# The end of the last batch in an attention and gated-MLP kernel: another order of products, statistics and writes

## The chip, the cores and the metric

The kernel runs on one core of a Trainium2 chip. A core has a matrix engine (TensorE, PE in the profile), a vector engine (VectorE, DVE), a scalar engine (ScalarE, ACT), a general-purpose engine (GpSimd, POOL) and a sync engine (SyncE, SP) that here only issues transfers. They run side by side, each in its own fixed order, and wait for one another through semaphores. Sixteen DMA engines move data. The metric is the device time of one execution in microseconds (us), lower is better.

## The reference

There are 8 batches of 576 tokens. Attention with 8 heads of 64 keeps only the scores within `tau` of the row's maximum; its result, 512 wide, is the input x of a gated MLP:

```python
h = np.maximum(x @ w_in, 0.0)                      # 512 -> 1024
u, v = h[..., :512], h[..., 512:]
v_n = (v - mean(v)) / np.sqrt(var(v) + 1e-06)      # over the 512 features of a token
v_s = einsum('ts,bsd->btd', w_spatial, v_n) + b_spatial[None, :, None]
out = (u * v_s) @ w_out                            # 512 -> 512
```

The spatial product runs over the tokens, so no row of the output can be finished before all tokens of v_n are there.

## The kernel before

Attention is worked off in steps, each of a block of 128 tokens for two heads: scores on TensorE, the maximum on VectorE, the exponentials and masks on ScalarE and VectorE, a DMA transpose of the probabilities, and the product with v. The order is written out by hand: a string of short tokens for each batch (`ORDER`) and four strings for the end (`LAST`). A token names one piece of work, and `run_token` (the long `elif` chain) emits its instructions at that place on whichever engines it uses. After the colon stands how many batches back it belongs to. The MLP of a batch runs in the gaps of the attention of the next two, but the last batch has no attention to hide behind: its MLP is `last_gmlp`, and the tokens of `LAST` are emitted around its parts, which are separated by `yield`.

The pieces that matter here:

- `P`, `i` and `p` are the product with v, the reciprocal of the row sums (L531) and the normalised rows xn (L534, VectorE). xn is held in two halves of four heads each, m = 14 and m = 15 for the last batch.
- `X0` sends the half m = 14 through a DMA transpose issued on SP (L555) and gives the contraction parts 0 and 1 of xT. `XP2`, `XP3` (L576) transpose the half m = 15 on TensorE, and `xp2`, `xp3` evict it with ScalarE (L416, L584) and VectorE (L585): parts 2 and 3 of xT.
- `o0` to `o3` are the last but one batch's output products (L767). `eo0` to `eo3` evict them (L778, even blocks on ScalarE, odd ones on VectorE) and issue the write on SP (L782). `s4` and `es4` are its spatial product for the last 64 tokens and the gating of it (L743, L755, VectorE).
- `u0` to `u4` and `eu0` to `eu4` are the last batch's u products (L709, L714) and their Relu on ScalarE (L412).

`last_gmlp` makes, block by block of 128 tokens (c = 0 to 3, and c = 4 with 64), the value product over four contraction parts f (L934; L627 for block 4, together with the output of the previous batch's last 64 rows, L630, in `ends`), its Relu on ScalarE (L941), mean and variance with bn_stats and bn_aggr on VectorE (L943, L945), and 1/sqrt on GpSimd in two calls (L957). After the next `yield` it forms the normalised values vn (L965, L968, L971). Then come the spatial products, `gate`, on half a bank of 256 tokens at a time (L982), each followed by VectorE's multiplication with u (L984), `gate_rest` for the last 64 tokens (L991), and the output products (L1001) with ScalarE's copy (L1003) and a write (L1004) from SP or, for odd blocks, from GpSimd's queue. `output_halves` does the last 64 rows as two halves whose writes are issued on SP and ScalarE (L1019).

The results of matmuls lie in eight banks, handed out in turn by `bank()`: six of one pool and two of another. A bank can be written again only when its last reader is done.

Of the kernel before, what the change touches and what calls it, by code (L numbers as in the profile page):

```python
# [9 lines left out]
F32 = mybir.dt.float32  # L10
BF16 = mybir.dt.bfloat16
# [4 lines left out]
ALU = mybir.AluOpType  # L16
ACT = mybir.ActivationFunctionType
# [145 lines left out]
    "C15:1 es1:2 OUT3:3 A15:1 E17:1 T13:1 s3:2 "),  # L163
(
# [3 lines left out]
(  # L168
    "u0:1 eu0:1 u1:1 eu1:1 "),
(  # L170
    "u2:1 eu2:1 u3:1 eu3:1 u4:1 eu4:1 ")]
WAYS = [
    "nananaanananaaanaa",
    "naaaaanananaaanaaa",
# [10 lines left out]
def kernel(  # L185
# [17 lines left out]
    nc = tc.nc  # L203
    B, H, S, D = q.shape
    assert (B, H, S, D) == (8, 8, 576, 64)
    scale = 0.125
# [3 lines left out]
    P = 128  # L210
# [3 lines left out]
    small = ctx.enter_context(tc.tile_pool(name="small", bufs=6))  # L214
# [3 lines left out]
    vr = ctx.enter_context(tc.tile_pool(name="vr", bufs=4))  # L218
    orr = ctx.enter_context(tc.tile_pool(name="orr", bufs=1))
    oo = ctx.enter_context(tc.tile_pool(name="oo", bufs=2))  # L220
    sqr = ctx.enter_context(tc.tile_pool(name="sqr", bufs=1))
# [12 lines left out]
    mhalf = const.tile([P, 1], F32, name="mhalf")  # L234
# [23 lines left out]
    w_in = const.tile([P, 4, 1024], BF16, name="w_in")  # L258
# [128 lines left out]
    def bank(dtype=F32, n=512):  # L387
        if wide:

            turn[0] += 1  # L390
            if turn[0] % 8 not in (2, 3):
                return wide[0].tile([P, n], dtype, name="t")
        return ps_f.tile([P, n], dtype, name="f")
# [164 lines left out]
    def x_of(b, f, cols):  # L558

        at = 640 * (f % 2)  # L560
        return xt_of(b)[:, f // 2, at + cols.start:at + cols.stop]
# [58 lines left out]
    us, gs = {}, {}  # L620
    pair_o = {}

    def ends(t, b):


        for f in range(4):
            nc.tensor.matmul(out=t[0:64], lhsT=rest_of(b, f), rhs=w_in[:, f, 512:1024],  # L627
                             start=(f == 0), stop=(f == 3))
            if b:
                nc.tensor.matmul(out=t[64:128], lhsT=gs[b - 1][:, f, 512:576],  # L630
                                 rhs=w_o[:, f, :], start=(f == 0), stop=(f == 3))
# [286 lines left out]
    def stage():  # L918

        t = ld_ring[len(staged) // 3 % 2][len(staged) % 3]  # L920
        half = len(staged) // 6 % 2
        staged.append(t)
        return t.rearrange("p h c d -> p (h c d)")[:, 512 * half:512 * half + 512]

    def last_gmlp(b):

        vn = vn_ring[b % 2]
        norms = []
        var = small.tile([P, 5], F32, name="var")
        vrel, mvs = [], []  # L930
        for c in range(5):
            t = bank()
            for f in range(4 if c < 4 else 0):
                nc.tensor.matmul(out=t, lhsT=x_of(b, f, slice(c * P, (c + 1) * P)),  # L934
                                 rhs=w_in[:, f, 512:1024], start=(f == 0), stop=(f == 3))
            if c == 4:
                ends(t, b)
            n = P if c < 4 else 64
            vrel.append(vr.tile([P, 512], F32, name="vrel") if c < 4 else
                        orr.tile([P, 512], F32, name="o"))  # L940
            nc.scalar.activation(out=vrel[c][:n], in_=t[:n], func=ACT.Relu)  # L941
            st = small.tile([P, 6], F32, name="st")
            nc.vector.bn_stats(out=st[:n], in_=vrel[c][:n])  # L943
            mvs.append(small.tile([P, 2], F32, name="mv"))
            nc.vector.bn_aggr(out=mvs[c][:n], in_=st[:n])  # L945
            if c == 4:
                nc.vector.memset(var[64:128, 4:5], 1.0)
                o = stage()
                nc.scalar.copy(out=o[64:128], in_=t[64:128])
                nc.sync.dma_start(out=out[b - 1, 512:576, :], in_=o[64:128])  # L950
            nc.vector.tensor_scalar(out=var[:n, c:c + 1], in0=mvs[c][:n, 1:2], scalar1=1e-6,
                                    scalar2=1.0, op0=ALU.add, op1=ALU.mult)
            if c in (2, 4):

                lo = 0 if c == 2 else 3
                rs = small.tile([P, 5], F32, name="rstd")
                nc.gpsimd.tensor_tensor(out=rs[:, lo:c + 1], in0=var[:, lo:c + 1],  # L957
                                        in1=mhalf.broadcast_to([P, c + 1 - lo]), op=ALU.pow)
                for d in range(lo, c + 1):
                    norms.append((d, rs[:, d:d + 1]))  # L960
        yield
        for d, rs in norms:
            n = P if d < 4 else 64
            nm = small.tile([P, 1], F32, name="nm")
            nc.vector.scalar_tensor_tensor(out=nm[:n], in0=mvs[d][:n, 0:1], scalar=-1.0,  # L965
                                           in1=rs[:n], op0=ALU.mult, op1=ALU.mult)
            if d == 3:
                nc.scalar.activation(out=vn[:n, d, :], in_=vrel[d][:n], func=ACT.Identity,  # L968
                                     scale=rs[:n], bias=nm[:n])
            else:  # L970
                (nc.gpsimd if d == 0 else nc.vector).tensor_scalar(  # L971
                    out=vn[:n, d, :], in0=vrel[d][:n], scalar1=rs[:n], scalar2=nm[:n],
                    op0=ALU.mult, op1=ALU.add)
        yield
        g = mw.tile([P, 4, S], BF16, name="gT")
        rows = out[b, 0:512, :].rearrange("(p c) n -> p c n", c=4)

        def gate(f, half):
            t = bank()
            cols = slice(256 * half, 256 * half + 256)  # L980
            for c in range(5):
                nc.tensor.matmul(out=t[:, 0:256], lhsT=vn[:, c, f * P:(f + 1) * P],  # L982
                                 rhs=wsT[:, c, cols], start=(c == 0), stop=(c == 4))
            nc.vector.tensor_tensor(out=g[:, f, cols], in0=t[:, 0:256], in1=us[b][:, f, cols],  # L984
                                    op=ALU.mult)

        def gate_rest():
            t = bank()
            for h in range(4):
                for c in range(5):  # L990
                    nc.tensor.matmul(out=t[:, h * 64:h * 64 + 64],  # L991
                                     lhsT=vn[:, c, h * P:(h + 1) * P],
                                     rhs=wsT[:, c, 512:576], start=(c == 0), stop=(c == 4))
            nc.vector.tensor_tensor(out=g[:, :, 512:576],
                                    in0=t[:, 0:256].rearrange("p (f s) -> p f s", f=4),
                                    in1=us[b][:, :, 512:576], op=ALU.mult)

        def output(c):
            t, o = bank(), stage()
            for f in range(4):  # L1000
                nc.tensor.matmul(out=t, lhsT=g[:, f, c * P:(c + 1) * P], rhs=w_o[:, f, :],  # L1001
                                 start=(f == 0), stop=(f == 3))
            nc.scalar.copy(out=o, in_=t)  # L1003
            (nc.sync, nc.gpsimd)[c % 2].dma_start(out=rows[:, c, :], in_=o)  # L1004

        def output_halves(c):
            ts, o = [bank(), bank()], stage()
            at = [slice(0, P)] * 2 if c < 4 else [slice(0, 64), slice(64, P)]
            n = P if c < 4 else 64
            for f in range(4):  # L1010
                for h in range(2):
                    nc.tensor.matmul(out=ts[h][at[h], 0:256], lhsT=g[:, f, c * P:c * P + n],
                                     rhs=w_o[:, f, 256 * h:256 * h + 256],
                                     start=(f == 0), stop=(f == 3))
            for h in range(2):
                cols = slice(256 * h, 256 * h + 256)
                (nc.scalar.copy, nc.vector.tensor_copy)[h](out=o[at[h], cols],
                                                           in_=ts[h][at[h], 0:256])
                (nc.sync, nc.scalar)[h].dma_start(  # L1019
                    out=rows[:, c, cols] if c < 4 else out[b, 512:576, cols], in_=o[at[h], cols])  # L1020

        for f in range(4):
            gate(f, 0)
        gate_rest()
        gate(0, 1)
        output(0)
        gate(1, 1)
        output(1)
        gate(2, 1)
        gate(3, 1)  # L1030
        output(2)
        output(3)
        output_halves(4)
        yield

# [175 lines left out]
```

## Time and profile before

| what | us |
|---|---|
| median of three runs | 437.54 |
| lowest and highest of them | 434.55 and 438.42 |
| the profiled execution, its own time | 439.63 |
| span of the profiled execution | 437.9 |
| transpose of xT, part 0 and 1: issued, landed | 409.22, 414.13 |
| first value product of the last batch | 414.18 |
| first and last bn_stats | 415.88, 420.05 |
| last matmul begins (output halves) | 432.37 |
| last writes issued | 433.37 to 433.52 |

The granted TensorE clock of the profiled execution is 0.994 of full speed. Three things help in reading its lines. A time is the start from the beginning of the span. In a line of the timeline the bracket gives how long the engine had been idle before and what ended that idle time; `x16` is a group of 16 instructions that follow one another. And the chain of work that ended last is walked back from the last instruction: at each step to whatever released it, or to the instruction before it on the same engine. Of the profiled span's last stretch, 433.1 to 437.9, nothing is computed any more; the last writes land and the program ends.

### The profile page before, as it was taken

The page shows a single profiled execution, that of the slowest core. Times are in us where ns is not written, and L with a number is a line of the kernel's source. Part 1 is how long each engine was busy: PE and PEld are TensorE (multiplying, and loading weights), DVE is VectorE, ACT ScalarE, POOL GpSimd, SP SyncE. Part 2 cuts the span into 40 slices and gives each one's busy share as a digit, 9 for nine tenths or more (in the row PEclk, how much of TensorE's full clock was granted, in tenths as well). Part 3 has the DMA queues.
Part 4 walks back from the last instruction along what each step waited for, and adds up shares of the span by engine and source line. Part 5 has one row for each costly group of instructions (what it writes and reads, how often), then busy time and mean ns, then how long its engine had stood idle before and what let it go on. Part 6 is the DMA issues. An engine that isn't in the chain of part 4 may idle for free.

```text
span 437.9 us, 12915 instructions
## 1 busy us (share of the span) xinstructions
PE 406.9 (93%) x4998; PEld 257.2 (59%) x5048; DVE 376.3 (86%) x689; ACT 383.5 (88%) x584; POOL 168.6 (39%) x374
## 2 busy tenths in 40 slices
PE   8778889989999999988999999999999999999895
PEld 4446655565755666565565666656656656555553
DVE  6889989898989889987889898988998998998482
ACT  4899989999999988998988999999999989998252
POOL 1244426583345611545233713356125621253021
PEclk9899999999999999999999999999999999999999
DMA  7999999999899999999989999999999997959803
GB/s 196 219 248 189 219 251 245 204 222 210 199 245 174 259 207 174 200 201 185 257 140 251 219 174 245 213 221 207 221 191 239 199 229 171 193 104 215 178 30 109
DMA packets 224637, 88.17 MB, mean 201 GB/s; under 512 B 195648, under 2 KB 220352, under 8 KB 224576
## 3 DMA queue, kind: packets, MB, share of 16 engines
q1 hardware_dynamic: 224048, 86.49, 97.6%
q8 instruction: 40, 0.66, 0.6%
q0 software_dynamic: 160, 0.52, 0.3%
q10 hardware_dynamic: 368, 0.33, 0.2%
q14 instruction: 21, 0.17, 0.1%
HBM read 32.79 MB, written 9.44 MB: 96 GB/s over the span
## 4 chain that ended last, share of the span: by engine, by line
PE 64%; ACT 12%; DVE 8%; DMA 6%; issue 5%; POOL 4%; SPq 1%; POOLq 0%; ACTq 0%; DVEq 0%
PE s L816 27%; PE f L738 6%; ACT e L874 5%; PE f L434 5%; PE f L496 5%; DVE s L850 5%; PE f L709 4%; PE f L642 4%; PE f L767 4%; DMA pT<-p 3%; ACT e L871 2%; ACT p L909 2%; PE f L491 2%; DMA xT<-xn 1%; PE f L627 1%
## 5 line engine op out<-in xcount | busy, mean ns | idle before, releaser
L850 DVE TENSOR_REDUCE s<-s 128x2 f32<-128x1152 f32 x144 | 196.2, 1362 | 22.3 <-PE s L816 18.7
L816 PE MATMUL s<-qkT 64*64 64x160 f32 (+1 forms) x2304 | 173.0, 418 | 13.3 <-ACT e L874 6.3
L816 PEld LDWEIGHTS s<-qkT 64*64 64x64 f32 x2304 | 107.6, 133 | 71.8 <-ACT e L874 18.1
L874 ACT ACTIVATE e<-s,negm 128x576 f32<-128x576 f32 x192 | 133.1, 744 | 9.6 <-DVE negm L856 7.1
L909 ACT ACTIVATE p<-e 128x1152 f16<-128x1152 f32 x96 | 111.6, 1173 | 0.7 <-PE s L816 0.2
L871 ACT ACTIVATE e<-s,negm 128x576 f16<-128x576 f32 x96 | 66.8, 746 | 6.4 <-DVE negm L856 4.5
L320 POOL CAST v<-vl 128x512 bf16<-128x512 f32 x32 | 20.2, 632 | 78.3 <-PE s L816 66.1
L496 PE MATMUL f<-v,pT 128*128 128x65 bf16 x984 | 44.6, 194 | 0.0
L496 PEld LDWEIGHTS <-pT 128*128 128x128 f16 x1024 | 41.9, 98 | 2.2 <-issue 0.2
L293 POOL COPY qn<-ql 128x512 f32<-128x512 f32 x31 | 20.4, 660 | 49.5 <-PE s L816 40.6
L902 DVE TENSOR_TENSOR p<-e 128x576 int32<-128x576 int32 x48 | 36.9, 772 | 0.7 <-PE s L816 0.5
L738 PE MATMUL f<-wsT,vn 128*128 128x512 bf16 x125 | 32.2, 380 | 0.4
L491 PE MATMUL f<-v,pT 128*128 128x130 bf16 x123 | 27.3, 222 | 3.9 <-DMA pT<-p 3.7
L694 POOL TENSOR_SCALAR vn<-vrel,rs,nm 128x512 bf16<-128x512 f32 (+1 forms) x35 | 28.4, 812 | 3.6
L709 PE MATMUL f<-xT,w_in 128*128 128x512 bf16 x100 | 28.6, 380 | 1.3 <-ACT qkT L414 0.3
L642 PE MATMUL f<-w_in,xT 128*128 128x512 bf16 x103 | 27.1, 380 | 0.5
L534 DVE TENSOR_TENSOR xn<-f,r 128x384 bf16<-128x384 f32 x46 | 24.9, 552 | 1.3 <-PE s L816 0.8
L446 POOL COPY qkT<-qkT 64x64 f32<-64x64 f32 x32 | 9.5, 296 | 42.6 <-PE s L816 17.9
L856 DVE TENSOR_SCALAR negm<-s 128x2 f32<-128x2 f32 x144 | 22.2, 154 | 4.0 <-PE s L816 1.5
L767 PE MATMUL f<-w_o,gT 128*128 128x512 bf16 x88 | 24.8, 380 | 0.7
L893 DVE TENSOR_SCALAR e<-e 128x1152 uint16<-128x1152 f16 x48 | 22.8, 476 | 0.1
L687 POOL TENSOR_TENSOR rs<-rs,mhalf 128x1 f32<-128x1 f32 (+1 forms) x35 | 21.2, 607 | 2.9
(162 smaller groups left out, 536.5 us busy)
## 6 DMA issues: line engine op xcount, KB each, us to landing
vl<-in_v_dram SPq DMA_DIRECT2D x16, 512.0 KB, 5.7
ql<-in_q_dram SPq DMA_DIRECT2D x15, 512.0 KB, 5.3
kl<-in_k_dram SPq DMA_DIRECT2D x15, 512.0 KB, 5.1
out_dram<-oo SPq DMA_DIRECT2D x12, 512.0 KB, 3.9
pT<-p SPq DMA_TRANSPOSE x141, 4.4
uT<-in_moe_w_in_dram SPq DMA_DIRECT2D x3, 512.0 KB, 4.6
uT<-in_moe_w_spatial_dram SPq DMA_DIRECT2D x2, 576.0 KB, 4.6
vx<-in_v_dram SPq DMA_DIRECT2D x16, 64.0 KB, 4.1
```

The costliest lines, as they stand in the source:

```text
L491: nc.tensor.matmul(out=t[:, at:at + 130], lhsT=pt[:, 4, rows], rhs=vt[:, 4:6, :].rearrange("p b d -> p (b d)"), start=True, stop=False)
L496: nc.tensor.matmul(out=t[:, at + 65 * h:at + 65 * h + 65], lhsT=pt[:, 5 * h + j, rows], rhs=vt[:, 6 * h + j, :], start=False, stop=(h == 1 ...
L642: nc.tensor.matmul(out=t, lhsT=x_of(b, f, slice(c * P, (c + 1) * P)), rhs=w_in[:, f, 512:1024], start=(f == 0), stop=(f == 3))
L709: nc.tensor.matmul(out=t, lhsT=w_in[:, m, f * P:(f + 1) * P], rhs=x_of(b, m, slice(0, 512)), start=(m == 0), stop=(m == 3))
L738: nc.tensor.matmul(out=t, lhsT=vn[:, c, f * P:(f + 1) * P], rhs=wsT[:, c, 0:512], start=(c == 0), stop=(c == 4))
L767: nc.tensor.matmul(out=t[:n], lhsT=gs[b][:, f, c * P:c * P + n], rhs=w_o[:, f, :], start=(f == 0), stop=(f == 3))
L816: made.append(nc.tensor.matmul(out=s_ring[g % 2][halves[k], at[h] + lo:at[h] + hi], lhsT=qks[n][halves[h], 0, m:m + 64], rhs=qks[n][halves ...
L850: nc.vector.tensor_reduce(out=nm[:, heads], in_=view(s_ring[g % 2], at[h0], dims), axis=AX.X, op=ALU.max, negate=True)
L871: nc.scalar.activation(out=half_e(g)[0][:, S * h:S * h + S], in_=s, func=ACT.Exp, bias=bias_, scale=scale if steps[g][1] == 4 else 1.0)
L874: nc.scalar.activation(out=e, in_=s, func=ACT.Prelu, bias=bias_, scale=scale if steps[g][1] == 4 else 1.0, alpha=1e30)
L902: nc.vector.tensor_tensor(out=numerators(g).bitcast(I32), in0=e.bitcast(I32), in1=kept.bitcast(I32), op=ALU.bitwise_and)
L909: nc.scalar.activation(out=numerators(g), in_=e_ring[g % 3].rearrange("p h s -> p (h s)"), func=ACT.Exp)
```

## The change

It has four parts.

1. In `LAST`, `eo1` moves from near the end of the second string to right behind `eo2`, and `es4` moves ahead of `XP2`. `u2` and `eu2` move from the fourth string to the third, so that they are emitted ahead of the making of vn.
2. The value products run parts 2 and 3 first for all four blocks, in four banks at once, then parts 0 and 1 block by block. Mean and variance of block 3 are no longer made by bn_stats: the Relu also gives the row sum, GpSimd makes the negative mean of it, and a Square on ScalarE gives the sum of squared differences. The var of blocks 0 to 2 is one instruction. vn of block 0 is made on VectorE and that of block 2 on GpSimd, where before it was the other way round.
3. The spatial products go over whole banks of 512 tokens, for f = 0 and 1 interleaved by block c, then for f = 2 and 3. The multiplications with u (`times`) follow behind all of them, and the four output products behind `gate_rest`.
4. The write of output block 3 is issued on SP and no longer on GpSimd. The copy and the write of the previous batch's last 64 rows go from the middle of the statistics to a place behind vn and the u evictions.

```diff
-    "P022:1 Z16:1 P101:1 P102:1 i10:1 i02:1 o1:2 T15:1 s4:2 P120:1 T16:1 i11:1 p02:1 T17:1 p11:1 deu4:2 eo2:2 "
-    "P121:1 p10:1 P122:1 o3:2 i12:1 p12:1 XP2:1 X0:1 XP3:1 xp3:1 xp2:1 eo1:2 o0:2 eo3:2 es4:2 deo0:2 "),
+    "P022:1 Z16:1 P101:1 P102:1 i10:1 i02:1 o1:2 T15:1 s4:2 P120:1 T16:1 i11:1 p02:1 T17:1 p11:1 deu4:2 eo2:2 eo1:2 "
+    "P121:1 p10:1 P122:1 o3:2 i12:1 p12:1 es4:2 XP2:1 X0:1 XP3:1 xp3:1 xp2:1 o0:2 eo3:2 deo0:2 "),
 (
-    "u0:1 eu0:1 u1:1 eu1:1 "),
+    "u0:1 eu0:1 u1:1 eu1:1 u2:1 eu2:1 "),
 (
-    "u2:1 eu2:1 u3:1 eu3:1 u4:1 eu4:1 ")]
+    "u3:1 eu3:1 u4:1 eu4:1 ")]
...
+        nc.vector.memset(var, 1.0)
+        nc.vector.memset(mv, 0.0)
...
+        ts = [bank() for _ in range(4)]
+        def product(c, f):
+            nc.tensor.matmul(out=ts[c], lhsT=x_of(b, f, slice(c * P, (c + 1) * P)),
+                             rhs=w_in[:, f, 512:1024], start=(f == 2), stop=(f == 1))
+        def stats(c):
+            n = P if c < 4 else 64
+            st = small.tile([P, 6], F32, name="st")
+            nc.vector.bn_stats(out=st[:n], in_=vrel[c][:n])
+            nc.vector.bn_aggr(out=mv[:n, c], in_=st[:n])
+        def power(lo, hi):
+            nc.gpsimd.tensor_tensor(out=rstd[:, lo:hi], in0=var[:, lo:hi],
+                                    in1=mhalf.broadcast_to([P, hi - lo]), op=ALU.pow)
+        def apply(eng, c):
+            n = P if c < 4 else 64
+            eng.tensor_scalar(out=vn[:n, c, :], in0=vrel[c][:n], scalar1=rstd[:n, c:c + 1],
+                              scalar2=shift[:n, c:c + 1], op0=ALU.mult, op1=ALU.add)
+        for f in (2, 3):
+            for c in range(4):
+                product(c, f)
+        total = small.tile([P, 1], F32, name="sm")
+        for c in range(4):
+            for f in (0, 1):
+                product(c, f)
+            if c < 3:
+                nc.scalar.activation(out=vrel[c], in_=ts[c], func=ACT.Relu)
+                stats(c)
+            else:
+                nc.scalar.activation(out=vrel[c], in_=ts[c], func=ACT.Relu, accum_out=total)
+        nc.vector.tensor_scalar(out=var[:, 0:3], in0=mv[:, 0:3, 1], scalar1=1e-6, scalar2=1.0,
+                                op0=ALU.add, op1=ALU.mult)
+        t = bank()
+        ends(t, b)
+        nc.scalar.activation(out=vrel[4][:64], in_=t[:64], func=ACT.Relu)
+        nmean = small.tile([P, 1], F32, name="nmean")
+        nc.gpsimd.tensor_scalar(out=nmean, in0=total, scalar1=-1.0 / 512, scalar2=0.0,
+                                op0=ALU.mult, op1=ALU.add)
+        nc.scalar.activation(out=sq, in_=vrel[3], func=ACT.Square, bias=nmean, accum_out=ss)
+        power(0, 3)
+        stats(4)
+        nc.vector.tensor_scalar(out=var[:64, 4:5], in0=mv[:64, 4, 1:2], ...)
+        nc.vector.tensor_scalar(out=var[:, 3:4], in0=ss, scalar1=1.0 / 512, scalar2=1e-6, ...)
+        power(3, 5)
         yield
+        nc.vector.scalar_tensor_tensor(out=shift[:, 0:3], in0=mv[:, 0:3, 0], scalar=-1.0,
+                                       in1=rstd[:, 0:3], op0=ALU.mult, op1=ALU.mult)
+        apply(nc.vector, 0)
+        nc.vector.tensor_tensor(out=shift[:, 3:4], in0=nmean, in1=rstd[:, 3:4], op=ALU.mult)
+        apply(nc.vector, 1)
+        apply(nc.gpsimd, 2)
+        nc.scalar.activation(out=vn[:, 3, :], in_=vrel[3], func=ACT.Identity, ...)
+        nc.vector.scalar_tensor_tensor(out=shift[:64, 4:5], in0=mv[:64, 4, 0:1], ...)
+        apply(nc.vector, 4)
         yield
+        o = stage()
+        nc.scalar.copy(out=o[64:128], in_=t[64:128])
+        nc.sync.dma_start(out=out[b - 1, 512:576, :], in_=o[64:128])
...
+        def gate(f, c):
+            if f not in gated:
+                gated[f] = bank()
+            nc.tensor.matmul(out=gated[f], lhsT=vn[:, c, f * P:(f + 1) * P],
+                             rhs=wsT[:, c, 0:512], start=(c == 0), stop=(c == 4))
+        def times(f, cols):
+            nc.vector.tensor_tensor(out=g[:, f, cols], in0=gated[f][:, cols],
+                                    in1=us[b][:, f, cols], op=ALU.mult)
...
-            (nc.sync, nc.gpsimd)[c % 2].dma_start(out=rows[:, c, :], in_=o)
+            (nc.gpsimd if c == 1 else nc.sync).dma_start(out=rows[:, c, :], in_=o)
...
-        for f in range(4):
-            gate(f, 0)
+        for c in range(5):
+            for f in (0, 1):
+                gate(f, c)
+        for f in (2, 3):
+            for c in range(5):
+                gate(f, c)
+        for f in range(3):
+            times(f, slice(0, 512))
+        for half in range(2):
+            times(3, slice(256 * half, 256 * half + 256))
         gate_rest()
-        gate(0, 1)
-        output(0)
-        gate(1, 1)
-        output(1)
-        gate(2, 1)
-        gate(3, 1)
-        output(2)
-        output(3)
+        for c in range(4):
+            output(c)
         output_halves(4)
```

More of the change, by code (lines that the diff above doesn't have):

```diff
@@ L927, in last_gmlp @@
         vn = vn_ring[b % 2]
-        norms = []
         var = small.tile([P, 5], F32, name="var")
[L930 to L937, printed above, removed]
+        rstd = small.tile([P, 5], F32, name="rstd")
@@ new lines, in last_gmlp @@
+        shift = small.tile([P, 5], F32, name="shift")
+        mv = small.tile([P, 5, 2], F32, name="mvs")
+        nc.vector.memset(var, 1.0)
+        nc.vector.memset(mv, 0.0)
+        vrel = [vr.tile([P, 512], F32, name="vrel") if c < 4 else orr.tile([P, 512], F32, name="o")
+                for c in range(5)]
+        ts = [bank() for _ in range(4)]
+        def product(c, f):
+            nc.tensor.matmul(out=ts[c], lhsT=x_of(b, f, slice(c * P, (c + 1) * P)),
+                             rhs=w_in[:, f, 512:1024], start=(f == 2), stop=(f == 1))
@@ L938, in last_gmlp @@
+        def stats(c):
             n = P if c < 4 else 64
-            vrel.append(vr.tile([P, 512], F32, name="vrel") if c < 4 else
-                        orr.tile([P, 512], F32, name="o"))
-            nc.scalar.activation(out=vrel[c][:n], in_=t[:n], func=ACT.Relu)
             st = small.tile([P, 6], F32, name="st")
             nc.vector.bn_stats(out=st[:n], in_=vrel[c][:n])
-            mvs.append(small.tile([P, 2], F32, name="mv"))
-            nc.vector.bn_aggr(out=mvs[c][:n], in_=st[:n])
@@ L946, in last_gmlp @@
[L946 to L960, printed above, removed]
@@ L961, in last_gmlp @@
-        yield
[L962 to L973, printed above, removed]
+            nc.vector.bn_aggr(out=mv[:n, c], in_=st[:n])
@@ new lines, in last_gmlp @@
+        t = bank()
[4 more added lines that the diff above has]
+                                op0=ALU.mult, op1=ALU.add)
+        sq = sqr.tile([P, 512], BF16, name="sq")
+        ss = small.tile([P, 1], F32, name="ss")
+        nc.scalar.activation(out=sq, in_=vrel[3], func=ACT.Square, bias=nmean, accum_out=ss)
@@ new lines, in last_gmlp @@
+        power(0, 3)
+        stats(4)
+        nc.vector.tensor_scalar(out=var[:64, 4:5], in0=mv[:64, 4, 1:2], scalar1=1e-6, scalar2=1.0,
+                                op0=ALU.add, op1=ALU.mult)
+        nc.vector.tensor_scalar(out=var[:, 3:4], in0=ss, scalar1=1.0 / 512, scalar2=1e-6,
+                                op0=ALU.mult, op1=ALU.add)
+        power(3, 5)
+        yield
+        nc.vector.scalar_tensor_tensor(out=shift[:, 0:3], in0=mv[:, 0:3, 0], scalar=-1.0,
+                                       in1=rstd[:, 0:3], op0=ALU.mult, op1=ALU.mult)
@@ new lines, in last_gmlp @@
+        apply(nc.vector, 0)
+        nc.vector.tensor_tensor(out=shift[:, 3:4], in0=nmean, in1=rstd[:, 3:4], op=ALU.mult)
+        apply(nc.vector, 1)
+        apply(nc.gpsimd, 2)
+        nc.scalar.activation(out=vn[:, 3, :], in_=vrel[3], func=ACT.Identity,
+                             scale=rstd[:, 3:4], bias=shift[:, 3:4])
+        nc.vector.scalar_tensor_tensor(out=shift[:64, 4:5], in0=mv[:64, 4, 0:1], scalar=-1.0,
+                                       in1=rstd[:64, 4:5], op0=ALU.mult, op1=ALU.mult)
@@ L974, in last_gmlp @@
+        apply(nc.vector, 4)
         yield
+        o = stage()
+        nc.scalar.copy(out=o[64:128], in_=t[64:128])
+        nc.sync.dma_start(out=out[b - 1, 512:576, :], in_=o[64:128])
         g = mw.tile([P, 4, S], BF16, name="gT")
         rows = out[b, 0:512, :].rearrange("(p c) n -> p c n", c=4)
[L978 to L985, printed above, removed]
+        gated = {}
```

## The prediction

> **What bounds the kernel now.** I read four views. The page's busy rows come first: TensorE (PE) is busy 93% of a 437.9 us span, ScalarE (ACT) 88%, VectorE (DVE) 86%, at a granted clock of 0.994. Averages of that kind say nothing about a change that touches only the last 30 us, so the second view is the chain that ended last, in order of time, from 408 us on. Its lines are start, duration, what:
>
> ```profile
> 408.67 0.44 issue
> 409.11 0.11 DVE xn L534
> 409.22 4.91 DMA xT<-xn
> 414.13 0.05 issue
> 414.18 1.05 PE t L934 x4
> 415.23 0.02 issue
> 415.25 0.61 ACT vrel L941
> 415.86 0.02 issue
> 415.88 0.71 DVE st L943
> ...
> 423.12 0.14 DVE nm L965 x2
> 423.25 0.02 issue
> 423.27 0.82 ACT vn L968
> 424.09 0.05 issue
> 424.14 0.94 PE t L982 x7
> ```
>
> The reader should see three stages. From 409.22 to 414.13 everything waits for one DMA transpose, the first half of the last batch's xT. From 415.88 to 421.3 DVE runs five rounds of statistics. Then the normalised values vn are made, and ACT's block 3, at 423.27, is the last that the first spatial product needs. From 424.14 the matmuls run almost without a gap to 433.0. The third view, the timeline, shows what TensorE lost to the first two stages (start, duration, engine, line, then in brackets the idle time before):
>
> ```profile
> 409.22 1.30 SPq L555 DMA_TRANSPOSE xT<-xn  x1
> 413.53 0.34 SPq L782 DMA_DIRECT2D out_dram<-kl  x1
> 414.18 3.63 PE L934 MATMUL t<-w_in,xT 128*128 128x512 bf16 x16 [1.20 <-DMA xT<-xn]
> 419.14 0.87 POOL L957 TENSOR_TENSOR rstd<-var,mhalf 128x3 f32<-128x3 f32 x1 [20.39 <-DVE var L951]
> 424.14 0.94 PE L982 MATMUL t<-wsT,vn 128*128 128x256 bf16 x7 [0.68 <-ACT vn L968]
> 424.91 1.25 PE L982 MATMUL f<-wsT,vn 128*128 128x256 bf16 x10
> ```
>
> PE idles 1.20 us before the value products. Before the spatial products only three matmuls (422.89 on) fit between 422.65, where the u products end, and 424.14: 1.49 less three times 0.109 is about 1.16 us idle. These two gaps are all the change can win on PE without removing work. The fourth view, stretches of time, confirms it: PE is busy 3.75 of the 3.80 us after 424.2 and 4.99 of the 5.10 us after 428.0.
>
> **The change part by part.** All before 409 us keeps its order on every engine.
>
> *The moved token eo1* (the ScalarE/VectorE eviction of output block 1 of batch 6, and its write). It issues a DVE copy (L778, 0.68 us, next DVE instruction 0.60 after its start) and an SP write of 256 KB. The copy passes two xn products, a reciprocal, the xT copy L585 and, with es4, L755. On SP the write passes the transpose X0. Before, X0 was issued at 409.22, as the xn product ended. Now SP first waits for the copy. On DVE that follows the u eviction (L406 at 409.58), so it starts at 409.91, where xn ran, and ends at 410.59; its matmuls ended at 409.18. The write issues at 410.62 for 0.34; adjacent SP issues stand 0.1 apart (414.13+0.33 to 414.56 is 0.1), so the transpose issues at 411.05, 1.83 us later.
>
> How long does it take to land? The nearest row is its own, 4.91 us. In 0.05 us slices of the DMA view its data moves from 410.4 to 411.95 at about 215 GB/s, after the earlier transfers drain at 410.3, and 2.1 us pass until it is seen. Moved, it stands behind the new write, whose data should start 0.9 after issue (kl: issued 413.53, data from 414.35) and take 0.7 us at 380 GB/s, until 412.2; the transpose's own data would start 411.05+1.2 = 412.25. So I keep 4.91: landing at 415.95. The 15 transposes of this line landed in 3.2 to 6.8 us (median 4.5), which bounds it to 414.25 and 417.85. Here a page speaks differently. The Trainium skill, DMA: Bandwidth & Descriptors, section on the fixed cost of one DMA and its table of measured limits, gives about 2.0 us fixed, and 261 GB/s for a transpose: 0.295 MB would land in 2.0+1.13 = 3.1 us, at 414.2, and the sum below would end near -2.8 us. The row has 4.91 for this very transfer, so the row decides; the rule is the good end of the range.
>
> *Delay of the PE transposes of the other half.* The two xn products behind the copy: the first runs at 410.51 to 411.07, still before PE takes it at 411.44 (PE is in o3 until then); the reciprocal then starts at 410.98 instead of 410.78, the last xn ends near 411.76 instead of 411.57. XP3 and o0 move by 0.15. es4 (0.41) fits on DVE while it waits for ACT's L584 (0.98 idle there before). Half 2,3 of xT is in place at 413.2.
>
> *Value products by contraction part.* Eight of the sixteen (parts 2, 3) now run from 413.2, at 0.217 each (16 in 3.63 with a tail of 0.16), to 414.95: inside the wait, 1.0 us before the transpose lands. That cover is not full to the brim, so the cost there is zero. After landing (PE starts at 416.0, as 414.13 gave 414.18) only eight remain, 1.74 us, saving 1.74. Block 0 is ready 2x0.217+0.2 after, at 416.63.
>
> *Statistics.* DVE now runs four rounds, not five, and one var row for blocks 0 to 2. Cycle before: 1.0 to 1.08 with var; without var I take 0.9. bn_stats at 417.26 (relu 0.60 first), the third round ends at 419.97, var to 420.17; POOL's power for three (0.87) to 421.08; bn_stats of block 4 and its two var rows fill DVE to 421.27. ScalarE: four Relu rows at 0.62 pitch, the accumulator read of the fourth (0.23, row L651), Relu of block 4 to 419.9, nmean on POOL (0.19) under it, Square 0.72+0.20 (rows L675) to 420.85. So var of block 3 does not wait. Second power 0.70, to 422.0. Two memsets on DVE fall at 413 to 414 in idle time.
>
> *vn.* Block 0 on DVE 421.5 to 422.05 (0.55). Shift 3 waits for the second power, 422.25. Block 1 on DVE beside POOL's block 2: the same pair before took 1.00 and 0.77 (alone 0.55), so 423.2 and 422.8. ACT's block 3, queued behind u0, u1, u2 (three at 0.60 from 420.85): 422.65 to 423.46. Block 4 to 423.85. Before, the last needed block came at 424.09.
>
> *PE from landing.* 416.0 + 1.74 products, +1.0 ends (417.73 to 418.72 before), +3.46 u0 to u3, +0.47 u4 = 422.67, where vn 0 is ready. Gates over whole banks go by c for f 0 and 1: c 1 wanted at 423.10, there at 423.25, a stall of 0.15; c 2 to c 4 are there when asked for (423.7, 424.1, 424.55). Whole banks: 20 at 0.217 = 4.34. Forty half banks cost 0.109 each (ten in 1.09 by the chain), 4.36. So the wide form is worth 0.02, nothing; the 20 weight loads that go were hidden under the matmuls. gate_rest 0.58, four outputs 3.47. Halves begin at 422.67+0.15+4.34+0.58+3.47 = 431.2. Before: 432.37. The gating products on DVE (0.69 each; last halves 0.42) end at about 427.8 for f 3, before output 0 takes its fourth part at 428.4; gate_rest covers them. If that cover went, 0.4.
>
> *Output tail.* Write 3 goes from POOL (0.56 issue) to SP (0.33). The end was set by the two half writes (issued 433.42 and 433.52, landing 3.0 later), and SP issues write 3 before its half in the gap while ACT copies: 0. The copy of the previous batch's last rows (L949, 0.58) moves behind u4 on ACT: it frees a bank for gate f 3, wanted at 426.1, free at 425.1; its write has 10 us.
>
> **Sum.** +1.82 (later landing), -1.74 (eight products ahead), -1.16 idle before the gates, +0.15 new stall, about -0.15 of small gaps (ends 0.08, outputs 0.1): -1.1 us. Against the profiled execution: span 437.9 to 436.8, its own time 439.63 to 438.5. That execution lies 2.1 above the median 437.54, so on the median: 436.4.
>
> **The rivals.**
> *The transpose decides against it (slower).* Every us of landing moves the end by one, as PE works without a gap afterwards. Break-even is a landing at 417.05, 6.0 us after issue. For: X0 now stands behind a write on the queue, and the same page (queues, rings and completion order) says each DMA engine takes one queue's descriptors in ring order, which no run here has shown for this pair; 6.8 is the slowest of the 15. Against: the queues are nearly empty then. Price at 6.8: 417.85, +0.8, so 438.3.
> *DVE stays the bound.* If the statistics cycle stays at 1.06 as in the old rounds, vn comes 0.5 later, and c 1 stalls 0.65 instead of 0.15: -0.6, 436.9.
> *Landing by the page's rule or the fast rows (3.2).* -2.8: 434.7. The profile is against it: no queue in front at 410.4, and still 4.91.
> *It does nothing measurable.* The three runs spread from 434.55 to 438.42, more than any of these sums.
>
> **How the numbers follow.** Forecast (-0.5 to -2) 0.57; slower rival (0 to +2) 0.22; early landing 0.12; unforeseen shift elsewhere, either sign, 0.09. The range takes the landing bounds (-2.8, +0.8) and part of the spread of runs (-3.0, +0.9 round the median): 433.5 to 439.0. For the likeliest case alone: 434.5 to 437.5. About 1% (4.4 us) is what a measurement of this kernel tells from no change. Faster by more needs a run spread on top of an early landing: 0.07. Slower by more needs a landing over 10 us after issue or an unforeseen cost: 0.06. Within: 0.87.
>
> **What would show it.** The transpose issued near 411.05, after the kl write, landing near 416; eight value matmuls before that; PE with less than 0.4 us idle between landing and the last output; third statistics round ending near 420; gates from 422.7. Wrong would be: a landing earlier than 414.5 or later than 417, PE waiting over 0.5 us for vn 1 to 4 or for gT in output 0, or a difference that arises before 409 us.

## The result, and the profile after

The changed kernel is a little faster: 435.48 us as the median of 22 runs (433.91 to 438.58) against 438.45 for the kernel before in as many runs (434.55 to 441.12). The ratio is 0.9947, with a 95% interval of 0.9925 to 0.9969: about 2.3 us less, between 1.4 and 3.3. It is taken between the means of the fast runs, without the one slow run of 441.12, so it is not quite the ratio of the medians. The forecast was 1.1 us less.

The two profiled spans, 437.9 and 433.6 us, differ by 4.3 us, and that is not all the change's. The paired reciprocals ahead of the last xn products (L531) begin at 408.33 before and at 406.41 after: 1.92 us had already gone apart where the order of work is the same in both. So from here on the tail is counted from the start of these reciprocals, in two stretches, up to the first matmul of the output halves and from there to the end of the span:

| kernel | transpose issued | landed | first output half | from there to the end | tail |
|---|---|---|---|---|---|
| before | 0.89 | 5.80 | 24.04 | 5.53 | 29.57 |
| after | 2.66 | 6.76 | 22.00 | 5.19 | 27.19 |

The tail is 2.38 us shorter. It is one execution of each kernel, and it agrees with the 2.3 of the many runs. Of it 2.04 us lie ahead of the output halves and 0.34 behind them. The chain that ended last, after (start, duration, what):

```profile
409.07 4.10 DMA xT<-xn
413.17 0.05 issue
413.21 1.90 PE t L939 x8
415.12 0.33 PE f L627
...
419.66 0.47 PE t L714 x16
420.12 2.16 PE t L1011 x10
422.28 2.16 PE f L1011 x10
424.44 0.58 PE t L1022 x20
425.02 3.45 PE t L1032 x16
```

The reader should see that the statistics and the making of vn are gone from the chain. From the landing to the end of the output products every step is a TensorE step, and each begins where the one before ended. The timeline of the same kernel shows the two places where the old gaps were:

```profile
408.69 0.33 SPq L782 DMA_DIRECT2D out_dram<-kl  x1
...
409.07 2.51 SPq L555 DMA_TRANSPOSE xT<-xn  x1
...
411.17 3.95 PE L939 MATMUL t<-w_in,xT 128*128 128x512 bf16 x16
...
419.00 0.77 POOL L954 TENSOR_SCALAR vn<-vrel,rstd,shift 128x512 bf16<-128x512 f32 x1
419.04 0.16 DVE L991 TENSOR_TENSOR shift<-nmean,rstd 128x1 f32<-128x1 f32 x1
419.12 0.93 DVE L954 TENSOR_SCALAR vn<-vrel,rstd,shift 128x512 bf16<-128x512 f32 x1
...
419.33 0.80 ACT L994 ACTIVATE vn<-vrel,shift,rstd 128x512 bf16<-128x512 f32 x1
...
419.96 2.32 PE L1011 MATMUL t<-wsT,vn 128*128 128x512 bf16 x10
...
420.03 0.86 ACT L412 ACTIVATE uT<-t 128x512 bf16<-128x512 f32 x2
420.14 0.54 DVE L954 TENSOR_SCALAR vn<-o,rstd,shift 64x512 bf16<-64x512 f32 x1
```

The write `kl` (that of eo1) now stands ahead of the transpose. The value products take 3.95 us for what took 3.63, so TensorE waits 0.3 us between the early eight and the rest, where it had idled 1.20 before. And block 1 of vn ends at 420.05, about 0.3 us before the third gate, the first that needs it, starts at 420.39 (419.96 and two gates of 0.216), so the gates run without a stall.

### The profile page after: what moved, and what is told of

The parts are those of the page before. It is cut to its first block, busy times and chain, and to the rows that moved or that the text cites. A ratio compares the mean times of both kernels' runs of the same rounds, so it can differ in the third digit from the quotient of the medians.

```text
span 433.6 us, 12917 instructions
## 1 busy us (share of the span) xinstructions
PE 407.3 (94%) x5028; PEld 253.7 (58%) x5028; DVE 374.6 (86%) x681; ACT 383.9 (89%) x587; POOL 167.5 (39%) x374
## 4 chain that ended last, share of the span: by engine, by line
PE 64%; ACT 13%; DVE 8%; DMA 6%; issue 4%; POOL 3%; SPq 0%; ACTq 0%; DVEq 0%; POOLq 0%
PE s L816 26%; ACT e L874 6%; PE f L738 6%; DVE s L850 5%; PE f L496 5%; PE f L709 5%; PE f L434 4%; PE f L642 4%; PE f L767 4%; DMA pT<-p 3%; ACT p L909 2%; DMA xT<-xn 2%; ACT e L871 2%; PE f L491 2%; PE f L627 1%
## 5 line engine op out<-in xcount | busy, mean ns | idle before, releaser
L816 PEld LDWEIGHTS s<-qkT 64*64 64x64 f32 x2304 | 106.5, 131 | 71.3 <-ACT e L874 18.8
L709 PE MATMUL f<-xT,w_in 128*128 128x512 bf16 x116 | 29.7, 380 | 0.5 <-ACT qkT L414 0.3
```

The source lines that it names most:

```text
L709: nc.tensor.matmul(out=t, lhsT=w_in[:, m, f * P:(f + 1) * P], rhs=x_of(b, m, slice(0, 512)), start=(m == 0), stop=(m == 3))
L816: made.append(nc.tensor.matmul(out=s_ring[g % 2][halves[k], at[h] + lo:at[h] + hi], lhsT=qks[n][halves[h], 0, m:m + 64], rhs=qks[n][halves ...
```

## The experiments

Each was measured in five rounds beside the kernel before. Single runs spread by several us and the intervals reach 1.0 to 1.6 us to either side, so the ratios bear only on effects larger than that; the smaller ones are read from the tail of one profiled execution each. In this table the column "first output half" is its start, counted from the reciprocals.

| kernel | transpose: issue to landing | first output half | to the end | tail | ratio to before |
|---|---|---|---|---|---|
| after | 4.10 | 22.00 | 5.19 | 27.19 | 0.9947 [0.9925, 0.9969] |
| eo1 put back | 4.3 | 21.58 | 5.28 | 26.86 | 0.9910 [0.9879, 0.9942] |
| products by block | 3.84 | 23.47 | 5.21 | 28.68 | 1.0031 [0.9994, 1.0067] |
| five statistics | 4.25 | 22.67 | 5.18 | 27.85 | 0.9951 [0.9919, 0.9982] |
| half gates | 3.6 | 22.13 | 4.76 | 26.89 | 0.9940 [0.9910, 0.9970] |
| GpSimd write kept | 4.10 | 21.99 | 5.58 | 27.57 | 0.9939 [0.9908, 0.9970] |
| all writes on SP | 4.1 | 21.97 | 4.66 | 26.63 | 0.9927 [0.9901, 0.9954] |
| eo1 back, all on SP | 4.4 | 21.58 | 4.65 | 26.23 | 0.9920 [0.9893, 0.9948] |
| eo1 back, products by block | 4.4 | 22.22 | 5.28 | 27.50 | 0.9963 [0.9941, 0.9985] |
| before, eo1 moved | 4.59 | 25.50 | 5.50 | 31.00 | 1.0048 [1.0017, 1.0079] |
| before, block 3 written from SP | 4.94 | 24.06 | 4.69 | 28.75 | 0.9984 [0.9953, 1.0015] |

**The moved eviction, alone in the kernel before.** The edit is the one token:

```diff
-    "... deu4:2 eo2:2 "
-    "P121:1 ... xp3:1 xp2:1 eo1:2 o0:2 ..."
+    "... deu4:2 eo2:2 eo1:2 "
+    "P121:1 ... xp3:1 xp2:1 o0:2 ..."
```

> The kernel before with nothing but eo1 moved to behind eo2, as the change moves it. The tail runs from the first of the paired reciprocals (L531) to the end of the span: 29.57 us before. X0 is issued 1.85 us later. Theory 1 (the old 4.91 us to landing were partly a wait behind the transfers of the earlier transposes, which are over by then): landing 4.1 us after issue, that is 1.0 us later than before, and the tail 1.0 longer: 30.6 us, ratio near 1.002. Rival, as in the forecast (4.91 again): 1.83 longer, 31.4 us, ratio 1.004.

The chain of this kernel has this line:

```profile
407.76 4.59 DMA xT<-xn
```

The transpose was issued 1.77 us later and landed after 4.59 us, not 4.91, so 1.45 later in all. The output halves came 1.46 us later. One us of landing costs one us of the end in the kernel before, and this part of the change, by itself, is a loss of 1.43 us of tail; the ratio 1.0048 shows a loss too. The landing lies between what the two sides expected.

**The same eviction put back, in the changed kernel.** The edit is the reverse one.

> The changed kernel with eo1 put back behind xp2, so that the transpose X0 is issued on SP ahead of the write of output block 1 again. The tail is measured from the first of the paired reciprocals (L531) to the end of the span: 29.57 us before, 27.19 us in the changed kernel. Theory 1 (the tail is bound by TensorE from where the value products can run, and the eight early ones fill the wait): X0 is issued 1.85 us earlier and lands before the early products end, so the sixteen run from the eviction of xT without a pause; what is won is only the 0.3 us that TensorE still waited in the changed kernel, plus at most 0.2 for the earlier xn: tail 26.7 to 26.9, ratio to before near 0.993. Rival (each us of landing moves the end by one): tail 25.3 to 26.2. The landing itself: 4.9 us from issue if it is the queue of earlier transfers that counts, 4.1 us as in the changed kernel if it is not.

The chain of this kernel:

```profile
409.58 0.37 ACT xT L584
409.95 0.50 ACT xT L416
410.45 0.05 issue
410.50 3.63 PE t L939 x16
414.12 0.33 PE f L627
```

There is no transpose in it any more. All sixteen products follow the eviction of the TensorE half of xT, as theory 1 has it, and the tail is 0.33 us shorter, not 1 or 1.8. So by this trace the moved eviction costs a little in the changed kernel too; the early products hide most of the delay. The landing, 4.3 us after issue, was neither of the two values expected.

**The value products block by block again.** With eo1 where the change put it:

```diff
-                             rhs=w_in[:, f, 512:1024], start=(f == 2), stop=(f == 1))
+                             rhs=w_in[:, f, 512:1024], start=(f == 0), stop=(f == 3))
-        for f in (2, 3):
-            for c in range(4):
-                product(c, f)
...
-            for f in (0, 1):
+            for f in range(4):
```

> The changed kernel with its value products block by block over parts 0 to 3 again; nothing of it can run before the transpose has landed. Theory 1 (TensorE bounds from the landing on): eight products of 0.217 us come back behind the landing, tail 27.19 + 1.74 = 28.9 us, ratio to before near 0.998. Rival (the statistics on VectorE and the making of vn bound, and TensorE has slack there): under 0.8 us, tail below 28.0.

```profile
410.79 3.84 DMA xT<-xn
414.62 0.05 issue
414.67 3.63 PE t L939 x16
```

The output halves came 1.47 us later although this transpose landed 0.26 us sooner: 1.73 at equal landing, which is eight products of 0.217. So TensorE bounds the tail from the landing on. And with eo1 put back at the same time:

> The changed kernel with eo1 put back and the value products block by block over parts 0 to 3. With eo1 put back alone the transpose landed 0.5 us after the products could begin. Theory 1 (the early eight are worth only the wait that they fill): the stretch from the paired reciprocals to the output halves grows from 21.58 us by 0.5 to 0.6, to 22.1 or 22.2. Rival (they are worth 1.74 whatever the landing, or the earlier end of all four blocks costs or helps the statistics): over 22.8.

```profile
414.10 3.63 PE L939 MATMUL t<-w_in,xT 128*128 128x512 bf16 x16 [0.73 <-DMA xT<-xn]
```

The stretch grew by 0.64 us from that with eo1 put back alone, close to the 0.5 to 0.6 expected. So the early products are worth what they cover: 1.7 us of the wait that the moved eviction lengthened, 0.6 us of the wait without it.

**Variance of block 3 on VectorE again.**

```diff
-                nc.scalar.activation(out=vrel[c], in_=ts[c], func=ACT.Relu, accum_out=total)
+            nc.scalar.activation(out=vrel[c], in_=ts[c], func=ACT.Relu)
...
-        nc.scalar.activation(out=sq, in_=vrel[3], func=ACT.Square, bias=nmean, accum_out=ss)
         power(0, 3)
+        stats(3)
```

> The changed kernel with the variance of block 3 by bn_stats and bn_aggr on VectorE again (no row sum, no Square on ScalarE). VectorE gets 0.80 us more ahead of the second power. Theory 1 (TensorE bounds, and vn is wanted block by block from 12.9 us after the paired reciprocals began): vn 1 comes about 0.4 us after it is asked for, so the tail grows by 0.3 to 0.5, to 27.5 to 27.7 us. Rival (VectorE is the bound): the whole 0.8, tail 28.0.

```profile
419.90 0.93 DVE L954 TENSOR_SCALAR vn<-vrel,rstd,shift 128x512 bf16<-128x512 f32 x1
...
419.95 0.60 PE L1004 MATMUL t<-wsT,vn 128*128 128x512 bf16 x2
...
420.90 1.90 PE L1004 MATMUL t<-wsT,vn 128*128 128x512 bf16 x8 [0.35 <-DVE shift L989]
```

Two gates run and then TensorE waits for block 1: the third would follow at 420.38 (two at 0.217) and starts at 420.90, 0.52 late. Block 1 of vn, the first line, ends at 420.83 here (the bracket names the VectorE instruction that overlaps its end). The stretch grew by 0.67, of which 0.15 is the later landing in this run. That is theory 1's mechanism, a little above its 0.3 to 0.5, and the tail of 27.85 lies between the two sides. The size fits the changed kernel: of the 0.80 us of VectorE work about 0.3 went into the time by which block 1 was early there, and the other 0.5 is the stall.

**The spatial products over half banks again,** in the order of before.

> The changed kernel with the spatial products over half banks in the order of before (four first halves, the rest, then second halves between the outputs). Theory 1: a half bank costs 0.109 us and a whole one 0.217, so the width is worth nothing, and what is lost is that block 4 of vn is asked for 0.43 us after block 0 instead of 1.74: tail up by 0.1 to 0.3, to 27.3 to 27.5 us. Rival (each matmul has a cost of its own, twenty fewer are worth 0.5 us or more): tail 27.7 or above.

```profile
420.25 1.61 PE L1010 MATMUL t<-wsT,vn 128*128 128x256 bf16 x10
420.44 0.54 DVE L954 TENSOR_SCALAR vn<-o,rstd,shift 64x512 bf16<-64x512 f32 x1
...
421.02 1.64 PEld L1010 LDWEIGHTS <-vn 128*128 128x128 bf16 x16 [0.41 <-DVE vn L954]
...
421.69 1.25 PE L1010 MATMUL f<-wsT,vn 128*128 128x256 bf16 x10
```

The second ten follow one another as fast as before; the first ten take 1.44 us from start to start of the next group instead of 1.09, because the weight load of block 4 waits for VectorE, which makes that block last. From the first gate to the output halves it is 8.89 us against 8.45. The end is 0.43 us shorter, though, and that gives it all back. The half-bank order puts gates between the outputs, so the four block writes leave over 4.3 us instead of 2.6. The tail came out at 26.89, below what either side expected, because this transpose also landed 0.4 to 0.5 us sooner than in the changed kernel and TensorE had no wait for it (0.3 us); at equal landing the order is worth about nothing.

**Which queue the last writes stand in.** Three kernels, one line each. The first, shown here, puts block 3 on GpSimd's queue again in the changed kernel. The second is the reverse edit in the kernel before. The third has `nc.sync` for every block in the changed kernel, so that no write is on GpSimd:

```diff
-            (nc.gpsimd if c == 1 else nc.sync).dma_start(out=rows[:, c, :], in_=o)
+            (nc.sync, nc.gpsimd)[c % 2].dma_start(out=rows[:, c, :], in_=o)
```

> The changed kernel with the write of output block 3 on GpSimd's queue again. The stretch from the first matmul of the output halves to the end of the span took 5.19 us in the changed kernel. Theory 1 (the write from GpSimd's queue ends last): 5.5 us. Rival, as in the forecast: 5.2, no change.

> The kernel before with nothing but the write of output block 3 issued on SP instead of GpSimd. The stretch from the first matmul of the output halves to the end of the span took 5.53 us before and 5.19 in the changed kernel. Theory 1 (the write from GpSimd's queue ends last): 0.3 us shorter, 5.2. Rival, as in the forecast (the two half writes end last): 5.5, no change.

> The changed kernel with the write of output block 1 on SP as well, so that GpSimd issues no write. The stretch from the first matmul of the output halves to the end of the span was 5.19 us in the changed kernel, where the two half writes landed 2.6 and 2.8 us after issue, and 4.69 and 4.76 in the two kernels with only block 1's write on GpSimd and the outputs 1.4 us apart, where they landed in 2.1 and 2.3. Theory 1 (the GpSimd write of block 1, issued 0.6 us before the last writes now that outputs follow at 0.86 us, shares the DMA engines with them): 4.7 to 4.8 us, half writes in 2.1 to 2.3. Rival (the closer spacing of the writes from SP is enough): 5.2 still.

The transfers of the last stretch (issuer, size, us from issue to landing) in the kernel before:

```profile
out_dram<-vl POOLq DMA_DIRECT2D x1, 256.0 KB, 2.8
out_dram<-ql SPq DMA_DIRECT2D x1, 64.0 KB, 3.0
out_dram<-ql ACTq DMA_DIRECT2D x1, 64.0 KB, 3.0
```

In the changed kernel:

```profile
out_dram<-ql POOLq DMA_DIRECT2D x1, 256.0 KB, 2.9
out_dram<-kl SPq DMA_DIRECT2D x1, 256.0 KB, 2.9
out_dram<-vl SPq DMA_DIRECT2D x1, 256.0 KB, 2.8
out_dram<-ql SPq DMA_DIRECT2D x1, 64.0 KB, 2.6
out_dram<-ql ACTq DMA_DIRECT2D x1, 64.0 KB, 2.8
```

In the changed kernel with block 3 on GpSimd as well:

```profile
out_dram<-vl POOLq DMA_DIRECT2D x1, 256.0 KB, 2.9
out_dram<-ql SPq DMA_DIRECT2D x1, 64.0 KB, 3.1
out_dram<-ql ACTq DMA_DIRECT2D x1, 64.0 KB, 3.1
```

In the changed kernel with none on GpSimd:

```profile
out_dram<-vl SPq DMA_DIRECT2D x2, 256.0 KB, 2.5
...
out_dram<-ql SPq DMA_DIRECT2D x1, 64.0 KB, 2.1
out_dram<-ql ACTq DMA_DIRECT2D x1, 64.0 KB, 2.3
```

The two small half writes are issued 1.05 to 1.16 us after the first output half in all of them. They land in 3.0 to 3.1 us with block 3 on GpSimd, in 2.6 to 2.8 with block 1 alone there and the outputs close together, and in 2.1 to 2.3 with none there. The end stretch of the changed kernel follows: 5.58, 5.19, 4.66. In the kernel before it went from 5.53 to 4.69, with half writes of 2.1 and 2.3 us, when its last GpSimd write moved to SP. The end repeats closely in the other profiled executions: the five with the close outputs and block 1 alone on GpSimd have 5.18 to 5.28, and the four with none there, or with block 1's write issued 3 us before the halves, have 4.65 to 4.76. The rival "closer spacing alone" is out, as all writes on SP at 0.86 us spacing end in 4.66.

Theory 1 has the right sign and the wrong reason. Its reason was that the GpSimd write ends last, for a gain of 0.3 us; with block 3 on GpSimd that write lands 0.4 us before the last half write, and the gain in the kernel before was 0.84. What the runs show is that the half writes land later. The writes of blocks 2 and 3 on SP do too: 2.9 and 2.8 us in the changed kernel, 2.5 and 2.4 with none on GpSimd. Block 1's write is issued 1.9 us before the halves, not the 0.6 that the expectation has; 0.6 is to block 2's write. How the delay comes about in the DMA engines was not tested. By the ratio alone, the gain of 0.84 us in the kernel before could not be told from nothing (0.9953 to 1.0015), nor the loss of 0.39 with block 3 on GpSimd again (0.9939 against 0.9947).

**Both together.**

> The changed kernel with eo1 put back behind xp2 and all four block writes on SP. Theory 1 (both gains stand in different stretches and add): the stretch from the paired reciprocals to the output halves 21.6 us, as with eo1 put back alone, and 4.7 to 4.8 from there to the end, a tail of 26.3 to 26.4 against 29.57 before and 27.19 in the changed kernel; ratio to before near 0.992. Rival: 26.9, as with eo1 put back alone.

The tail is 26.23 us: the two gains stand in different stretches and add. By the trace this kernel has 3.34 us less tail than the kernel before and 0.96 less than the changed one. By time it beats the kernel before (0.9920), but its interval overlaps that of the changed kernel, so the runs do not rank these two.

## Why the prediction was right, and where its sum was off

The direction held, and so did the mechanism in the main: a later landing, eight products ahead of it, no idle before the gates. The forecast size was half of what was measured. The mis-sized terms are the landing (0.96 us and not 1.82), the end (0.34 less and not 0) and, by a little, the stretch before the gates. Step by step:

- *eo1 delays the transpose.* Issue was forecast 1.83 us later and was 1.77 later. The landing was mis-sized: the sum took 4.91 us, and it took 4.10, so the delay counted 0.96 and not 1.82. This is 0.86 of the 1.3 us missing. The row of before was taken as the transfer's own time, and it is not that: the same transfer took between 3.6 and 4.94 us in twelve kernels, and 3.6 to 4.25 in the changed kernel and the five variants whose work is the same up to this point. The 3.1 us worked out from the Trainium skill (DMA: Bandwidth & Descriptors, the fixed cost under Anatomy of one DMA and the transpose rate under Latency and other measured facts) was too short in all of them; the page fits that fixed cost to transfers issued from GpSimd, and this one is issued on SP. What the landing waited for is read below.
- *Eight products ahead of the landing, 1.74.* Confirmed at 1.73. Between the end of these eight and the landing the forecast had 1.0 us of wait; 0.3 us remained.
- *The idle 1.16 us before the gates goes, a stall of 0.15 comes.* The idle went and the stall did not come. From the start of the small u products to the output halves it took 10.19 us before and 8.91 after: 1.28 less, where the sum had 1.16 with its small gaps. Statistics rounds ran at about 0.8 us, not 0.9, so block 1 was 0.3 us early. The rival with VectorE as the bound falls. Without the Square on ScalarE a stall of 0.52 us was left, so that part of the 1.28 is shown; the earlier u2, the exchange of vn 0 and 2 and the later copy were not run by themselves.
- *Whole banks are worth nothing.* Right for the matmuls (0.216 against twice 0.109). What was overlooked is the order that comes with them: it saves about 0.4 us of stall at the gates and pushes the writes together, which costs 0.4 at the end while block 1's write is on GpSimd.
- *Output tail, 0.* Wrong: moving block 3's write off GpSimd is worth 0.39 us in the changed kernel and 0.84 in the kernel before, and the closer outputs take about 0.5 of the 0.84 back (5.53 to 4.69 to 5.19). The step that failed is "the end was set by the two half writes (issued 433.42 and 433.52, landing 3.0 later)": they do set it, but the 3.0 us was not theirs; it was 2.1 to 2.3 without a GpSimd write near them. (Before, the copies for these writes run until 433.49, so the stretch in which nothing is computed begins there and not at 433.1.)
- *The rivals.* The slower one had the right price, 1:1 in the kernel before (1.46 for 1.45), and its condition, a landing over 6.0 us after issue, did not occur. In the changed kernel the price runs only down to the end of the early products. The rival of an early landing has the nearest number, -2.8, but not its reason: 3.2 us did not occur. The rival of no measurable effect falls with the interval, which ends at 0.9969.

With the measured terms: +0.96 - 1.74 - 1.28 - 0.34 is -2.4 us, the tail's 2.38.

The DMA packets show what the landing waited for. In the view of them the GB/s row has 40 equal slices of the window. The first two lines are of before from 412.0 to 414.4, the last two of after from 409 to 411. The times of single packets below are from the same two traces.

```profile
GB/s 4 290 0 0 0 0 0 0 0 0 0 0 0 0 0 0 0 0 0 0 0 0 0 0 0 0 0 0 0 0 0 0 0 0 0 0 0 0 0 205
q8 instruction: 1, 0.02, 2.4%
...
GB/s 0 0 328 0 0 0 0 0 0 0 287 123 451 410 287 451 205 451 451 246 410 287 451 246 123 41 0 0 41 0 0 0 41 0 0 0 41 0 0 0
q8 instruction: 1, 0.02, 4.0%
```

In before the transpose's data have moved by 412.1. What runs then is one 16 KB packet of the instruction queue (q8), from 412.11 to 413.05. Of the 32 packets of 4 bytes that close the transpose, 30 came by 411.95 and the last two at 413.03 and 413.05, and the landing follows 1.1 us later.

In after such a packet runs from 409.14 to 410.43, during the write of eo1. Of this write's 16 closing packets 15 came by 410.34; its last data packets follow singly (the 41 in the row), and the sixteenth closing packet comes at 411.45. The data of the transpose run from 411.47 to 412.67, so they begin 2.4 us after issue where the forecast had 1.2, and the landing follows 0.5 us after them where it had 2.1. So the write ahead held the transpose back, as the slower rival feared; in five of the seven kernels with this order its data begin within 0.06 us of the write's last packet. That the forecast still came within 0.8 us of the landing is luck.

All twelve executions have such a packet at this place, 0.92 to 1.42 us long. That it holds up one DMA engine, and with it the transfer, is read from these times; no run moves it, so the cause is not shown by experiment. One difference stays open: the transpose's data moved in 1.6 to 1.7 us in the three kernels with the old end and in 1.2 where it ran without a pause in the others.

## What to carry to other kernels

A stage that starts with the data at hand is worth the wait it covers, no more: the same eight matmuls were worth 1.7 us behind a delayed transfer and 0.6 us when the transfer was not delayed by an eviction placed ahead of it. So before paying for cover, look at which instruction is queued ahead of the transfer. At the end of a program, read the landing times of the last small writes and not only their issue: they may carry the time of another queue's transfer. And the time of one transfer in one profile is not its own until its packets have been looked at.

## What the runs showed of the hardware that was not expected

- A 256 KB write from GpSimd's queue near the end lengthened the landing of two 64 KB writes on other queues: 2.1 to 2.3 us without it or with it issued 3 us earlier, 2.6 to 2.8 with it issued 1.9 us earlier, 3.0 to 3.1 with it issued beside them.
- The DMA transpose's own issue on SP took 1.29 to 1.30 us where the last write ahead of it on SP had been issued 0.9 to 1.2 us before it, and 2.04 to 2.63 us where that was 0.4 us.
- One 16 KB packet of the instruction queue took 0.92 to 1.42 us. In each of the five kernels without a write just ahead of the transpose, the transpose's last two closing packets came 0.9 to 1.1 us after the other 30; in four of the five they came within 0.02 us of the end of the instruction packet.
